# Down-projection phases of a fused attention and GLU kernel: halves with six weight buffers, or thirds with seven, and where the weight loads are placed

## The chip, the core and the metric

The kernel runs on one core of one Trainium2 chip. The metric is the device time of one execution in microseconds (us); lower is better.

## The reference

Four blocks follow each other on 2048 tokens of width 576, each with a layer norm ahead of it and a residual sum behind it. Blocks one and three are attention, blocks two and four a gated linear unit; both attention blocks share their weights, and so do both GLU blocks.

```python
def _A_ref(x, wqkv, wo):            # H = 32 heads of 18, window W = 8, dilation 2
    q, k, v = split(x @ wqkv)
    idx = pos[:, None] - arange(W) * 2
    logits = einsum("bhsd,bhswd->bhsw", q, k[idx]) * 18 ** -0.5     # masked where idx < 0
    o = einsum("bhsw,bhswd->bhsd", softmax(logits), v[idx])
    return merge_heads(o) @ wo

def _B_ref(x, w_gate, w_up, w_down):  # 576 -> 4608 -> 576
    return ((x @ w_gate) * (x @ w_up)) @ w_down

x = x + _A_ref(_layernorm(x), A_wqkv, A_wo)
x = x + _B_ref(_layernorm(x), B_w_gate, B_w_up, B_w_down)
x = x + _A_ref(_layernorm(x), A_wqkv, A_wo)
x = x + _B_ref(_layernorm(x), B_w_gate, B_w_up, B_w_down)
```

## The kernel before

**Steps.** The 16 token tiles of 128 go in two groups of eight, layer after layer. A step `j` is one attention and one GLU for one or two tiles (`nst`); the first four steps have one tile, the other 14 have two, 18 in all. Gate and up weights (`wg`, `wu`, `wgu_t`) stay in SBUF; the down weights (`wd`) are read again from HBM in every step, 18 loads of 288 KB a step.

**Order.** Nothing is issued where the source stands. Every piece of work is recorded by `op` with its engine, an assumed cost, and the keys that it reads and writes; `Plan.run` then issues all of them greedily by assumed start time, and that order is each engine's instruction stream. An engine works through its stream in order. A dependency exists where a key was written or read by an operation recorded *earlier*. The planner assumes a cost for DMAs too (`nbytes`, `late`), one queue at a time. The GLU matmuls of all steps form one chain (`bb`), so the attention's operations are fitted in between.

**The GLU.** A unit is 512 columns of gate and up: for two tiles, two of the 36 feature tiles, so 18 units a step. Three units form a group: `full` (L709) does the 128-row parts, `tails` (L720) the last 64 rows, into PSUM banks `pg` and `pu`, three of each. `evac` copies the gate to SBUF on ScalarE (L731) and multiplies on VectorE (L732); the result `h` goes into one of `NH` = 9 buffers. A bank is free again when that product is done. After nine units, a half (`nph` = 2 for two tiles), a down phase multiplies them by `wd` (L756, L757) into one bank of each kind and `acct`, and `settle` (L766, L771) adds the sums to the residual `xf`. One-tile steps have nine units and three phases of three.

**The loads.** There are `NWD` = 6 buffers `wd`. The first six loads are issued by SP, all others by GpSimd. In `glu`, the loads of three units are recorded ahead of their gate/up matmuls:

```python
for m in us:
    wsl[m] = [load_wd(m * fpu // 2 + g) for g in range(fpu // 2)]
...
for m in mine:
    down(m, hsl[m], wsl[m], ph, use)
```

All nine loads of a half are so recorded ahead of its down matmuls. Loads seven to nine take the buffers of the first three, and their only recorded dependency is on those loads and on the half before. They are issued as soon as that half's matmuls have freed the buffers.

**The attention.** `esel` (L568) sums the products of queries and keys per head, the softmax follows on VectorE and ScalarE (L590 to L601). Its weights must be spread over the partitions: from step 5 on L621 writes them to `a_dram`, and four reads at L624 bring them back as `ab`, all by SP's queue, which also has the transposing DMAs at L387. VectorE then multiplies values by `ab` (L641) and adds (L655), and TensorE projects with `wo` (L668).

Of the kernel before, what the change touches and what calls it, by code (L numbers as in the profile page):

```python
# [9 lines left out]
ACT = mybir.ActivationFunctionType  # L10
# [7 lines left out]
                 "lat", "margin", "ready", "end", "nbytes", "use", "pair", "need", "due", "late")  # L18


SLACK = {"DVE": 500, "ACT": 300}


class Plan:
# [11 lines left out]
    def op(self, eng, cost, fn, r=(), w=(), prio=1, after=None, hold=None, free=None, margin=0, nbytes=0, use=None,  # L36
           pair=None, need=None, due=False, late=0):
        o = Op()
        o.due, o.late = due, late
        o.eng, o.cost, o.fn, o.prio, o.hold, o.free = eng, cost, fn, prio, hold, free  # L40
        o.margin, o.idx, o.succ, o.order, o.nbytes = margin, len(self.ops), [], set(), nbytes
        o.lat, o.use, o.pair, o.need = self.LAT[eng], use, pair, need
        d = set()
        for k in r:
            d.update(self.wr.get(k, ()))
        for k in w:
            d.update(self.wr.get(k, ()))
            d.update(self.rd.get(k, ()))
        for k in r:
            self.rd.setdefault(k, []).append(o)  # L50
        for k in w:
            self.wr[k] = [o]
            self.rd[k] = []
        d.discard(o)
        o.deps = d
        if after is not None and after not in d:
            o.order.add(after)
        for p in d | o.order:
            p.succ.append(o)
        o.n = len(d | o.order)  # L60
        self.ops.append(o)
        return o
# [80 lines left out]
def kernel(  # L143
# [12 lines left out]
    nc = tc.nc  # L156
    _, S, D = A_x.shape
    F = B_w_gate.shape[1]
    P = 128
# [10 lines left out]
    NFT = F // P  # L170
# [3 lines left out]
    qscale = float(Dh) ** -0.5  # L174
    assert D == 576 and TL == 64 and NTT % (2 * GT) == 0 and NFT % 4 == 0 and nlayers % 2 == 0

    NXS, NWD, NH, NXB, NB = 4, 6, 9, 3, 3

    consts = ctx.enter_context(tc.tile_pool(name="consts", bufs=1))
    psum = ctx.enter_context(tc.tile_pool(name="psum", bufs=1, space=PSUM))  # L180
# [3 lines left out]
    wd_v = B_w_down.rearrange("(g t p) d -> g p t d", p=P, t=2)  # L184
# [36 lines left out]
    wd = [sb(f"wd{i}", [P, 2, D]) for i in range(NWD)]  # L221
# [3 lines left out]
    acct = psum.tile([P, 512], FP32, name="acct")  # L225
# [5 lines left out]
    late = {}  # L231

    pl = Plan()
    op = pl.op
# [120 lines left out]
    def head(src, keys, nst, dst, key, prio, ab, on_pe, mg, c0=0):  # L355

        mv, st, rstd, nmr, xn = mv_[ab], st_[ab], rstd_[ab], nmr_[ab], xn_[ab]
        ia = c0 // P
        for i in range(nst):
            def stats(i=i):  # L360
                xr = src(i).rearrange("p (a b) -> p a b", a=2)
                for a in range(2):
                    nc.vector.bn_stats(out=st[:, ia + i, a, :], in_=xr[:, a, :])
                nc.vector.bn_aggr(out=mv[:, ia + i, :], in_=st[:, ia + i])
            op("DVE", 970, stats, r=[keys[i]], w=[f"mv{ab}{ia + i}"], prio=prio)
        mk = [f"mv{ab}{ia + i}" for i in range(nst)]
        nk = [f"nmr{ab}{ia + i}" for i in range(nst)]
        sl = slice(ia, ia + nst)

        def rs():  # L370
            nc.scalar.activation(rstd[:, sl], mv[:, sl, 1], ACT.Ln, bias=eps_t[:])
            nc.scalar.activation(rstd[:, sl], rstd[:, sl], ACT.Exp, scale=-0.5)
        rk = [f"rstd{ab}{ia + i}" for i in range(nst)]
        op("ACT", 440, rs, r=mk + ["eps"], w=rk, prio=prio)
        op("DVE", 75, lambda: nc.vector.scalar_tensor_tensor(nmr[:, sl], mv[:, sl, 0], -1.0, rstd[:, sl], op0=ALU.mult, op1=ALU.mult),
           r=mk + rk, w=nk, prio=prio)
        for i in range(nst):
            def apply(i=i):
                x, y = src(i), xn[ia + i]
                sc = dict(bias=nmr[:, ia + i:ia + i + 1], scale=rstd[:, ia + i:ia + i + 1])  # L380
                nc.scalar.activation(y[:, 0:D], x, ACT.Identity, **sc)
                if not on_pe:
                    nc.scalar.activation(y[:, D:D + TL], x[:, KF * P:D], ACT.Identity, **sc)
            op("ACT", 770 if on_pe else 1100, apply, r=[keys[i], nk[i]], w=[f"xn{ab}{ia + i}"], prio=prio)
            cs = slice(c0 + i * P, c0 + (i + 1) * P)
            if not on_pe:
                op("SP", 1250, lambda i=i, cs=cs: nc.sync.dma_start_transpose(out=dst[:, :, cs], in_=xn[ia + i][:]),  # L387
                   r=[f"xn{ab}{ia + i}"], w=[key + str(ia + i)], prio=0, nbytes=P * KT * P * 2, late=3000)
                continue
            b = Bank()  # L390

            def tr(i=i, b=b):
                for k in range(KF):
                    nc.tensor.transpose(bf(b())[:, k, :], xn[ia + i][:, k * P:(k + 1) * P], ident[:])
                for r_ in (0, TL):
                    nc.tensor.transpose(bf(b())[r_:r_ + TL, KF, :], xn[ia + i][:, KF * P:D], ident[:])
            o = op("PE", 290, tr, r=[f"xn{ab}{ia + i}", "ident"], prio=0, margin=mg, **b.take())
            pl.also(o, [key + str(ia + i)])
            op("ACT", 590, lambda i=i, b=b, cs=cs: nc.scalar.copy(dst[:, :, cs], bf(b())), r=[b.key], w=[key + str(ia + i)],  # L399
               prio=prio, **b.drop())  # L400
# [277 lines left out]

    chain = {"pe": None}
    unit_no = {"n": 0}  # L680
    wd_no = {"n": 0}

    def fkeys(nm, fts):
        return sorted({f"{nm}{ft * FS // NFT}" for ft in fts})
# [1 line left out]
    def glu(j, t0, nst, last):  # L686
        n = nst * P
# [11 lines left out]
        def bb(eng, cost, fn, **kw):  # L699
            o = op(eng, cost, fn, prio=1, after=chain["pe"], **kw)  # L700
            chain["pe"] = o
            return o
# [30 lines left out]
               r=[f"wu_{j}_{u}", f"g{gs}"], w=[f"h{hs}"], prio=0, due=True, free="unit", use=use)  # L733
            return hs

        def load_wd(g):
            b = wd_no["n"] % NWD
            wd_no["n"] += 1
            first = wd_no["n"] <= NWD
            eng, q = ("SP", nc.sync) if first else ("POOL", nc.gpsimd)  # L740
            op(eng, 550 if first else 1100, lambda: q.dma_start(wd[b][:], wd_v[g]), w=[f"wd{b}"], nbytes=P * 2 * D * 2, late=0 if first else 1000,  # L741
               prio=5.5 + (g // 3 if j == 0 else 0))
            return b

        nph = 2 if nst == 2 else 3
        upp = nu // nph

        def down(u, hs, bl, ph, use):
            for e, ft in enumerate(fts(u)):
                first, fin = ft == ph * upp * fpu, ft == (ph + 1) * upp * fpu - 1  # L750

                def fn(e=e, ft=ft, first=first, fin=fin):
                    wt = wd[bl[e // 2]]
                    for i in range(nst):
                        lhs = hb[hs][:, e * n + i * P:e * n + (i + 1) * P]
                        nc.tensor.matmul((pg, pu)[i][use["slot"]][:], lhsT=lhs, rhs=wt[:, e % 2, 0:512], start=first, stop=fin)  # L756
                        nc.tensor.matmul(acct[:, i * TL:(i + 1) * TL], lhsT=lhs, rhs=wt[:, e % 2, 512:D],  # L757
                                         start=(first and i == 0), stop=fin, skip_group_check=True)
                kw = dict(hold="unit", use=use) if first else {}
                bb("PE", 245 * nst, fn, r=[f"h{hs}", f"wd{bl[e // 2]}"], w=["acc", "acct"], **kw)  # L760

        def settle(ph, use):
            fin = last and ph == nph - 1
# [12 lines left out]

        units = {}
        for ph in range(nph):
            hsl, wsl = {}, {}
            mine = range(ph * upp, (ph + 1) * upp)  # L780
            for u in range(ph * upp, (ph + 1) * upp, NB):
                us = (u, u + 1, u + 2)
                for m in us:
                    wsl[m] = [load_wd(m * fpu // 2 + g) for g in range(fpu // 2)]
                    units[m] = {}
                full(u, wg, "wg", pg, True, False, pair=tuple(units[m] for m in us))
                full(u, wu, "wu", pu, True, False)
                full(u + 1, wg, "wg", pg, True, False, need=units[u + 1])
                tails(us)
                hsl[u] = evac(u)  # L790
                full(u + 1, wu, "wu", pu, False, True)
                hsl[u + 1] = evac(u + 1)
                full(u + 2, wg, "wg", pg, False, True)
                full(u + 2, wu, "wu", pu, False, True)
                hsl[u + 2] = evac(u + 2)
            use = {"left": nst}
            for m in mine:
                down(m, hsl[m], wsl[m], ph, use)
            settle(ph, use)

    seq = []
# [13 lines left out]
    setup_b()  # L815
    setup_wo()
    setup_glu()
    for j, (l, t0, nst) in enumerate(seq):
        if l == 0 and j >= 4:
            load_x(t0, nst)  # L820
        pool["k"] = "pa" if j else "boot"
        attention(j, l, t0, nst)
        if j == 0:
            op("PE", 0, lambda: None, w=list(boot_keys), free="unit", use={"slot": NB - 1})
        glu(j, t0, nst, l == n_al - 1)
# [30 lines left out]
```

## Time and profile before

| | |
|---|---|
| median of 3 runs | 1116.48 us |
| lowest, highest | 1112.98, 1119.39 us |
| the profiled execution | 1110.56 us |
| its span | 1108.7 us |
| TensorE (PE) busy | 1058.9 us |
| VectorE (DVE) busy | 760.4 us |
| ScalarE (ACT), GpSimd (POOL) busy | 352.9, 242.7 us |
| read from HBM | 118.51 MB |
| mean granted TensorE clock | 0.99 |

Every duration below comes from the profiled execution, and its times are in us from the span's start unless marked ns. In the lists of waits a row names the engine and tile that waited, after the arrow the engine and tile that ended the wait, and then the total in us, the count and the longest. In timelines the brackets give the engine's idle time before the instruction and what ended it.

### The profile page before, as it was taken

The page shows a single profiled execution, that of the slowest core. Times are in us where ns is not written, and L with a number is a line of the kernel's source. Part 1 is how long each engine was busy: PE and PEld are TensorE (multiplying, and loading weights), DVE is VectorE, ACT ScalarE, POOL GpSimd, SP SyncE. Part 2 cuts the span into 40 slices and gives each one's busy share as a digit, 9 for nine tenths or more (in the row PEclk, how much of TensorE's full clock was granted, in tenths as well). Part 3 has the DMA queues.
Part 4 walks back from the last instruction along what each step waited for, and adds up shares of the span by engine and source line. Part 5 has one row for each costly group of instructions (what it writes and reads, how often), then busy time and mean ns, then how long its engine had stood idle before and what let it go on. Part 6 is the DMA issues. An engine that isn't in the chain of part 4 may idle for free.

```text
span 1108.7 us, 25201 instructions
## 1 busy us (share of the span) xinstructions
PE 1058.9 (96%) x10752; PEld 793.9 (72%) x10824; DVE 760.4 (69%) x1346; ACT 352.9 (32%) x704; POOL 242.7 (22%) x348
## 2 busy tenths in 40 slices
PE   6999999897989999999998999999999999999998
PEld 5777777775766677776776677777777777777775
DVE  7688989778787979888796533585877867322222
ACT  6633254331333353132332122225233232211211
POOL 4043433022202202222102222220222222222220
PEclk8999999998999999999999999999999999999999
DMA  9945654363336324463434334232343433333330
GB/s 302 284 162 172 196 155 129 87 125 115 90 56 144 88 69 120 121 135 108 97 90 121 119 97 120 68 122 54 121 121 109 118 87 121 99 102 114 98 119 31
DMA packets 84848, 132.74 MB, mean 120 GB/s; under 512 B 42048, under 2 KB 63744, under 8 KB 84736
## 3 DMA queue, kind: packets, MB, share of 16 engines
q0 software_dynamic: 25440, 93.80, 28.4%
q1 hardware_dynamic: 59296, 37.33, 13.6%
q8 instruction: 84, 1.38, 0.5%
q14 instruction: 28, 0.23, 0.1%
HBM read 118.51 MB, written 4.06 MB: 111 GB/s over the span
## 4 chain that ended last, share of the span: by engine, by line
PE 72%; DVE 16%; DMA 7%; issue 2%; ACT 1%; SPq 1%; POOL 0%; DVEq 0%; POOLq 0%; ACTq 0%
PE pu L709 18%; PE pg L709 18%; PE pg L756 9%; PE pu L756 7%; PE pg L720 5%; PE pg L455 5%; PE pu L455 3%; DVE prod L641 3%; PE pa L668 3%; PE acct L757 3%; DVE oT L655 3%; DMA ab<-a_dram 3%; DMA a_dram<-s 2%; DVE h L732 2%; DVE prod L553 2%
## 5 line engine op out<-in xcount | busy, mean ns | idle before, releaser
L741 POOL DMA_DIRECT2D wd<-in_B_w_down_dram x318 | 229.4, 723 | 836.2 <-PE acct L757 800.2
L731 ACT CAST g_sb<-pg 128x512 bf16<-128x512 f32 x288 | 158.9, 585 | 523.9 <-PE pu L720 361.9
L709 PE MATMUL pu<-xnT_B,wu 128*128 128x256 bf16 (+1 forms) x2592 | 301.6, 262 | 6.2 <-DVE h L732 6.2
L709 PE MATMUL pg<-xnT_B,wg 128*128 128x256 bf16 (+1 forms) x2592 | 300.5, 261 | 1.6 <-ACT xnT_B L399 1.6
L732 DVE TENSOR_TENSOR h<-pu,g_sb 128x512 bf16<-128x512 f32 x288 | 193.3, 685 | 139.2 <-ACT g_sb L731 87.1
L709 PEld LDWEIGHTS <-wu 128*128 128x128 bf16 x2592 | 224.3, 98 | 47.0 <-issue 23.6
L709 PEld LDWEIGHTS <-wg 128*128 128x128 bf16 x2592 | 229.1, 98 | 29.9 <-issue 1.5
L757 PE MATMUL acct<-wd,h 128*128 128x64 bf16 x1152 | 222.7, 193 | 4.0 <-issue 0.4
L756 PE MATMUL pg<-wd,h 128*128 128x512 bf16 x605 | 218.0, 382 | 0.1
L756 PEld LDWEIGHTS <-h 128*128 128x128 bf16 x1152 | 113.3, 98 | 132.7 <-issue 3.2
L756 PE MATMUL pu<-wd,h 128*128 128x512 bf16 x475 | 181.9, 383 | 6.7 <-DVE h L732 6.7
L757 PEld LDWEIGHTS <-h 128*128 128x128 bf16 x1152 | 113.3, 98 | 7.8 <-issue 6.9
L455 PEld LDWEIGHTS <-wqkv 128*128 128x128 bf16 (+1 forms) x1260 | 100.1, 101 | 26.0 <-issue 15.5
L553 DVE TENSOR_TENSOR prod<-qT,kv 128x2560 bf16<-128x2560 bf16 (+1 forms) x68 | 90.0, 1326 | 24.3 <-ACT kv L497 23.3
L655 DVE TENSOR_TENSOR oT<-oT,prod 128x1280 bf16<-128x1280 bf16 (+1 forms) x119 | 91.1, 765 | 3.6
L641 DVE TENSOR_TENSOR prod<-kv,ab 128x1280 bf16<-128x1280 bf16 (+1 forms) x120 | 88.3, 738 | 2.1 <-PE pg L646 1.9
L720 PE MATMUL pu<-xnT_B,wgu_t 64*128 64x256 bf16 (+1 forms) x648 | 80.5, 260 | 4.1 <-DVE h L732 3.8
L455 PE MATMUL pg<-xnT_A,wqkv 128*128 128x256 bf16 (+3 forms) x650 | 80.8, 267 | 2.5 <-DMA xnT_A<-xn 1.7
L720 PE MATMUL pg<-xnT_B,wgu_t 64*128 64x256 bf16 (+1 forms) x648 | 80.5, 260 | 0.0
L455 PE MATMUL pu<-xnT_A,wqkv 128*128 128x256 bf16 (+3 forms) x610 | 78.0, 268 | 0.1
L766 DVE TENSOR_TENSOR xf<-pg,xf 128x512 f32<-128x512 f32 (+1 forms) x40 | 27.3, 683 | 72.0 <-PE pg L756 70.8
L720 PEld LDWEIGHTS <-wgu_t 64*128 64x128 bf16 x1296 | 50.7, 94 | 28.4 <-issue 23.2
(99 smaller groups left out, 665.0 us busy)
## 6 DMA issues: line engine op xcount, KB each, us to landing
wd<-in_B_w_down_dram POOLq DMA_DIRECT2D x318, 288.0 KB, 4.5
ab<-a_dram SPq DMA_DIRECT2D x52, 128.0 KB, 2.8
wg<-in_B_w_gate_dram SPq DMA_DIRECT2D x6, 768.0 KB, 9.3
wu<-in_B_w_up_dram SPq DMA_DIRECT2D x6, 768.0 KB, 10.4
out_dram<-xf SPq DMA_DIRECT2D x8, 288.0 KB, 5.4
wraw<-in_A_wqkv_dram SPq DMA_DIRECT2D x4, 432.0 KB, 4.7
wd<-in_B_w_down_dram SPq DMA_DIRECT2D x6, 288.0 KB, 8.3
xb<-in_A_x_dram SPq DMA_DIRECT2D x6, 288.0 KB, 3.3
```

Of the source, the lines that this page charges most:

```text
L455: nc.tensor.matmul(bank(p_, u)[0:m, e * n:(e + 1) * n], lhsT=wqkv[r_, k, w0:w0 + m], rhs=xnT_A[r_, k, c0:c0 + n], start=start, stop=stop, ...
L553: nc.vector.tensor_tensor(late["prod"][p_ % 2][:, :, :, 0:n], q2, k2, op=ALU.mult)
L641: nc.vector.tensor_tensor(js(dst), js(vT[:, :, o0:o0 + n]), abw, op=ALU.mult)
L655: op("DVE", 70 + 2.63 * n, lambda i_=i_: nc.vector.tensor_tensor(oT[:, :, 0:n], oT[:, :, 0:n], late["prod"][i_ % 2][:, 0, :, 0:n], op=ALU. ...
L668: nc.tensor.matmul(b()[:, 0:HD], lhsT=oT[:, t, i * P:(i + 1) * P], rhs=wo_p[:, t, hh * HD:(hh + 1) * HD], start=(t == 0), stop=(t == KT - 1))
L709: nc.tensor.matmul(pt[:, e * n:(e + 1) * n], lhsT=w_[:, k, ft * P:(ft + 1) * P], rhs=xT[:, k, 0:n], start=(first and k == 0 and e == 0), s ...
L720: nc.tensor.matmul(ps[:, e * n:(e + 1) * n], lhsT=wgu_t[r_, ft * P:(ft + 1) * P], rhs=xT[r_, KF, 0:n], start=(first and e == 0), stop=not ...
L731: op("ACT", 490, lambda: nc.scalar.copy(g_sb[gs][:, 0:ul], pg[use["slot"]][:, 0:ul]), r=[f"wg_{j}_{u}"], w=[f"g{gs}"], prio=0, due=True)
L732: op("DVE", 605, lambda: nc.vector.tensor_tensor(hb[hs][:, 0:ul], pu[use["slot"]][:, 0:ul], g_sb[gs][:, 0:ul], op=ALU.mult), r=[f"wu_{j}_{ ...
L741: op(eng, 550 if first else 1100, lambda: q.dma_start(wd[b][:], wd_v[g]), w=[f"wd{b}"], nbytes=P * 2 * D * 2, late=0 if first else 1000, p ...
L756: nc.tensor.matmul((pg, pu)[i][use["slot"]][:], lhsT=lhs, rhs=wt[:, e % 2, 0:512], start=first, stop=fin)
L757: nc.tensor.matmul(acct[:, i * TL:(i + 1) * TL], lhsT=lhs, rhs=wt[:, e % 2, 512:D], start=(first and i == 0), stop=fin, skip_group_check=True)
```

## The change

Two-tile steps get three down phases of six units instead of two of nine (`nph = 3` for all steps), so `NH` = 6 buffers for `h` suffice. There are `NWD` = 7 buffers for down weights. A counter `used` walks through the buffers in the order of the down matmuls; when the two feature tiles of a load have been recorded, the next load into that buffer is recorded right behind them, so it depends on exactly these matmuls. Seven loads are recorded ahead of everything and go by SP, the other 317 by GpSimd. The operation that applies the layer norm (L381) is now also a reader of `rstd`.

```diff
+POOLQ = True
-    NXS, NWD, NH, NXB, NB = 4, 6, 9, 3, 3
+    NXS, NWD, NH, NXB, NB = 4, 7, 6, 3, 3
...
-            op("ACT", 770 if on_pe else 1100, apply, r=[keys[i], nk[i]], w=[f"xn{ab}{ia + i}"], prio=prio)
+            op("ACT", 770 if on_pe else 1100, apply, r=[keys[i], nk[i], rk[i]], w=[f"xn{ab}{ia + i}"], prio=prio)
...
-    wd_no = {"n": 0}
+    wd_no = {"n": 0, "used": 0}
+
+    def load_wd():
+        i = wd_no["n"]
+        wd_no["n"] += 1
+        if i >= len(seq) * NFT // 2:
+            return
+        b, first = i % NWD, i < NWD
+        eng, q = ("SP", nc.sync) if first or not POOLQ else ("POOL", nc.gpsimd)
+        op(eng, 550 if first else 1100, lambda: q.dma_start(wd[b][:], wd_v[i % (NFT // 2)]), w=[f"wd{b}"], nbytes=P * 2 * D * 2,
+           late=0 if first else 1000, prio=5.5 + (i // 3 if first else 0))
...
-        def load_wd(g):
-            b = wd_no["n"] % NWD
-            wd_no["n"] += 1
-            first = wd_no["n"] <= NWD
-            eng, q = ("SP", nc.sync) if first else ("POOL", nc.gpsimd)
-            op(eng, 550 if first else 1100, lambda: q.dma_start(wd[b][:], wd_v[g]), w=[f"wd{b}"], nbytes=P * 2 * D * 2, late=0 if first else 1000,
-               prio=5.5 + (g // 3 if j == 0 else 0))
-            return b
-
-        nph = 2 if nst == 2 else 3
+        nph = 3
...
-        def down(u, hs, bl, ph, use):
+        def down(u, hs, ph, use):
...
+                wb = wd_no["used"] % NWD
...
-                bb("PE", 245 * nst, fn, r=[f"h{hs}", f"wd{bl[e // 2]}"], w=["acc", "acct"], **kw)
+                bb("PE", 245 * nst, fn, r=[f"h{hs}", f"wd{wb}"], w=["acc", "acct"], **kw)
+                if e % 2:
+                    wd_no["used"] += 1
+                    load_wd()
...
-                    wsl[m] = [load_wd(m * fpu // 2 + g) for g in range(fpu // 2)]
...
+    for _ in range(NWD):
+        load_wd()
     for j, (l, t0, nst) in enumerate(seq):
```

More of the change, by code (lines that the diff above doesn't have):

```diff
@@ L734, in evac, with fn @@
             return hs
-        def load_wd(g):
-            b = wd_no["n"] % NWD
-            wd_no["n"] += 1
-            first = wd_no["n"] <= NWD
-            eng, q = ("SP", nc.sync) if first else ("POOL", nc.gpsimd)
-            op(eng, 550 if first else 1100, lambda: q.dma_start(wd[b][:], wd_v[g]), w=[f"wd{b}"], nbytes=P * 2 * D * 2, late=0 if first else 1000,
-               prio=5.5 + (g // 3 if j == 0 else 0))
-            return b
-        nph = 2 if nst == 2 else 3
+        nph = 3
         upp = nu // nph
-        def down(u, hs, bl, ph, use):
+        def down(u, hs, ph, use):
             for e, ft in enumerate(fts(u)):
                 first, fin = ft == ph * upp * fpu, ft == (ph + 1) * upp * fpu - 1
-                def fn(e=e, ft=ft, first=first, fin=fin):
-                    wt = wd[bl[e // 2]]
+                wb = wd_no["used"] % NWD
+                def fn(e=e, ft=ft, first=first, fin=fin, wb=wb):
+                    wt = wd[wb]
                     for i in range(nst):
@@ L778, in glu @@
         for ph in range(nph):
-            hsl, wsl = {}, {}
+            hsl = {}
             mine = range(ph * upp, (ph + 1) * upp)
@@ L797, in glu @@
             for m in mine:
-                down(m, hsl[m], wsl[m], ph, use)
+                down(m, hsl[m], ph, use)
             settle(ph, use)
```

## The prediction

> **What bounds the kernel now.** I read the page first, then the waits, then the timelines of DVE, SP and POOL around the longest TensorE waits, and at last the windows behind them. `h` is the product that DVE writes at L732; the bounce is the DMA round trip by which the attention weights are spread over partitions (L621 writes `a_dram`, four reads at L624 bring it back as `ab`).
>
> ```profile
> span 1108.7 us, 25201 instructions
> PE 1058.9 (96%) x10752; PEld 793.9 (72%) x10824; DVE 760.4 (69%) x1346; ACT 352.9 (32%) x704; POOL 242.7 (22%) x348
> ```
>
> TensorE is busy for 96%. Its work is the same before and after, so only the 50 us in which it stands still, and what follows from them, are to be had. The waits name their causes:
>
> ```profile
> PE pu L756 <- DVE h L732: 6.7, 2, 5.6
> PE pu L709 <- DVE h L732: 6.2, 2, 3.5
> PE pu L720 <- DVE h L732: 3.8, 2, 2.0
> PE pa L668 <- DVE xf L674: 3.4, 4, 1.5
> PE pa L668 <- DVE oT L655: 3.2, 4, 1.2
> DVE oT L641 <- DMA ab<-a_dram: 50.1, 12, 7.8
> ```
>
> Six waits for `h` make 16.7 us. Why is `h` late? Around the longest:
>
> ```profile
> 246.17 0.69 DVE L732 TENSOR_TENSOR h<-pu,g_sb 128x512 bf16<-128x512 f32 x1 [1.05 <-PE pu L709]
> 254.17 0.83 DVE L641 TENSOR_TENSOR oT<-kv,ab 128x1280 bf16<-128x1280 bf16 x1 [7.32 <-DMA ab<-a_dram]
> 257.25 1.28 DVE L732 TENSOR_TENSOR h<-pu,g_sb 128x512 bf16<-128x512 f32 x2
> ```
> ```profile
> 241.20 0.36 SPq L621 DMA_DIRECT2D a_dram<-s  x1
> 249.90 1.75 SPq L624 DMA_DIRECT2D ab<-a_dram  x4
> ```
> ```profile
> 228.72 0.72 POOL L741 DMA_DIRECT2D wd<-in_B_w_down_dram  x1 [33.49 <-PE acct L757]
> 233.62 2.16 POOL L741 DMA_DIRECT2D wd<-in_B_w_down_dram  x3 [0.26 <-PE acct L757]
> 236.96 0.72 POOL L741 DMA_DIRECT2D wd<-in_B_w_down_dram  x1 [1.18 <-DMA wd<-in_B_w_down_dram]
> ```
>
> DVE executes in order. The first multiplication by `ab` sits in its queue and waits 7.3 us for the bounce; the next `h`, whose PSUM bank has long been filled, stands behind it, and TensorE runs out of free banks. The bounce is late because nine down-weight loads went out in the 9 us from 228.7, ahead of it: the `a_dram` write alone took until 249.9. Without loads beside it the bounce takes 6.0 us (L601 ends at 403.97, `ab` is used at 410.01):
>
> ```profile
> 403.29 0.68 DVE L601 TENSOR_TENSOR s<-Lt,zs 128x512 bf16<-128x512 f32 x1
> 410.01 0.81 DVE L641 TENSOR_TENSOR oT<-kv,ab 128x1280 bf16<-128x1280 bf16 x1
> ```
>
> A long wait costs more than itself, since the granted clock falls to half behind it (the row after each wait; PE, PEld, DVE, ACT and POOL busy, then PEclk, DMA share, GB/s):
>
> ```profile
> 252.40:258.00 5.60, 0.03 (x2) 0.01 (x1) 3.79 (x6) 0.00 (x0) 0.00 (x0) 0.88 0.11 25
> 258.00:263.50 5.50, 5.28 (x22) 2.35 (x23) 5.43 (x8) 0.59 (x1) 0.00 (x0) 0.50 0.00 0
> 309.90:314.70 4.80, 4.76 (x34) 3.12 (x34) 4.73 (x7) 1.66 (x3) 0.00 (x0) 0.64 0.83 59
> 606.00:608.70 2.70, 0.04 (x1) 0.03 (x1) 2.67 (x5) 0.00 (x0) 0.00 (x0) 0.91 0.00 2
> 608.70:611.60 2.90, 2.90 (x14) 1.98 (x14) 2.90 (x5) 0.59 (x1) 0.00 (x0) 0.50 0.00 0
> ```
>
> Lost to the clock: 5.5 x 0.50 + 4.8 x 0.36 + 2.9 x 0.50 = 2.8 + 1.7 + 1.5 = 5.9 us. With the waits, **22.6 us** hang on late bounces, at five places: 4.5 us a place.
>
> The Trainium skill (TensorE: Matmul & The Clock Gate, Part 1: The HAM clock gate) has the clock fall after at least one idle window of about 3.4 us. The trace is stricter: 2.70 us were enough before 608.7. By the page's rule alone that place would have kept its clock, and the 22.6 us would be 21.1.
>
> **The change, part by part.** *Thirds instead of halves.* Each of the 14 two-tile steps gets one more down phase and one more settle. TensorE's matmuls stay; the question is the seam.
>
> ```profile
> 959.00:967.82 8.82, 8.71 (x72) 4.54 (x72) 0.76 (x2) 0.00 (x0) 3.40 (x5) 1.00 0.31 88
> 977.40:982.75 5.35, 5.35 (x50) 4.62 (x50) 2.08 (x3) 1.33 (x3) 0.00 (x0) 1.00 0.01 3
> ```
>
> A down of nine units takes 8.82 us, 0.98 a unit, and runs between two gate/up blocks with TensorE busy throughout; the 48 gate/up matmuls that follow each other across two groups of three units take 5.35. A third is thus two such groups and a down of 5.9 us, and the extra seam costs 0. What hides it: the last `h` of a third has 5 x 0.98 = 4.9 us of down matmuls ahead of it, against the 0.69 us of the `h` rows above and an ACT copy of a like size. If an `h` is late by more, it is the case counted below.
>
> ```profile
> L766 DVE TENSOR_TENSOR xf<-pg,xf 128x512 f32<-128x512 f32 (+1 forms) x40 | 27.3, 683 | 72.0 <-PE pg L756 70.8 <-PE acct L757 1.0
> L766 DVE TENSOR_TENSOR xf<-pu,xf 128x512 f32<-128x512 f32 (+1 forms) x28 | 19.1, 681 | 0.0
> L771 DVE TENSOR_TENSOR xf<-acct,xf 128x128 f32<-128x128 f32 (+2 forms) x40 | 10.6, 264 | 0.8
> ```
> ```profile
> 330.00:440.00 110.00, 105.02 (x984) 77.58 (x990) 92.91 (x163) 44.84 (x94) 19.47 (x27) 1.00 0.42 106
> ```
>
> The 14 settles add 14 x (0.68 + 0.68 + 0.26) = 23 us to DVE, which has 348 us idle. They stand in its queue where TensorE is in a down and no `h` is due (that row shows DVE waiting 70.8 us for down ends already). I take 0; at most the 1.6 us of a settle delay attention work in the stretch where DVE is busiest (92.9 us of the 110 above); five of the 14 steps run there, at some 65 us a step from 220 to 550: 8 us. Less than 0 is excluded, since they are added work.
>
> *The loads.* Their number stays 324, seven instead of six by SP at the start. Each is now placed behind the matmuls that free its buffer, so nothing is queued behind it on GpSimd but the next load.
>
> ```profile
> L741 POOL DMA_DIRECT2D wd<-in_B_w_down_dram x318 | 229.4, 723 | 836.2 <-PE acct L757 800.2 <-DMA wd<-in_B_w_down_dram 24.0 <-PE pa L668 7.1
> DMA to landing us min/median/max: 3.2/4.6/12.3
> ```
>
> A buffer freed in one third is read seven units on, behind at least the two gate/up groups of a third, 10.7 us; landing takes 4.6 us, at worst 12.3, and that in a burst of nine. So TensorE waits for no weight: 0, as before, where no wait for `wd` is listed. The seventh load by SP delays the last two of six gate/up slices by 1.4 us (0.29 MB at the 211 GB/s shown below); the first tile reads them in its last third: 0. `NH` 9 to 6 costs 0, since a third has six `h` and the next third's first comes behind all its downs. The added `rk` only lengthens a chain that `nmr` had already: 0.
>
> *The bursts.* This is the term that counts. A down now releases six loads in 5.9 us, not nine in 9. I read in the built program where each of the 13 bounces stands. Five begin inside a down, as at 296 before; three begin just behind one; five stand clear of any. In one of the first five the `ab` multiplication precedes the next `h` directly; in four, two `h` stand ahead of it.
>
> ```profile
> 295.25 0.69 DVE L601 TENSOR_TENSOR s<-Lt,zs 128x512 bf16<-128x512 f32 x1
> 307.73 0.82 DVE L641 TENSOR_TENSOR oT<-kv,ab 128x1280 bf16<-128x1280 bf16 x1 [7.04 <-DMA ab<-a_dram]
> 190.60 0.69 DVE L601 TENSOR_TENSOR s<-Lt,zs 128x512 bf16<-128x512 f32 x1
> 202.32 0.82 DVE L641 TENSOR_TENSOR oT<-kv,ab 128x1280 bf16<-128x1280 bf16 x1 [4.45 <-DMA ab<-a_dram]
> 588.41 0.69 DVE L590 TENSOR_REDUCE mx<-pa 128x64 f32<-128x512 f32 x1 [0.96 <-PE pa L568]
> 592.18 0.69 DVE L601 TENSOR_TENSOR s<-Lt,zs 128x512 bf16<-128x512 f32 x1
> ```
> ```profile
> DMA packets 1591, 3.17 MB, mean 211 GB/s; under 512 B 418, under 2 KB 1058, under 8 KB 1591
> ab<-a_dram SPq DMA_DIRECT2D x4, 128.0 KB, 7.0
> ```
>
> The second fence is the DMA of 294 to 309 us. The bounce there took 307.73 - 295.94 = 11.8 us with nine loads. Three loads fewer are 0.88 MB, 4.2 us at the 211 GB/s shown; they were issued together with the `ab` reads, so about half of that stood before these: 2.0 us less, **9.8 us**, between the quiet 6.0 and the 11.8. The direct case: 11.8 us gave a wait of 3.5, so it waits from 8.3 on: 1.5 us now, too short for the clock (bounds 0 and 5.2). The case with two `h` ahead: 202.32 - 191.29 = 11.0 gave 2.0, so it waits from 9.0 on where the bounce began 1 us before the next gate/up block. In three of the four, the `esel` matmuls stand 16 gate/up matmuls (1.8 us) and a down (5.9) ahead of that block; from `esel`'s end to L601's end is 4.5 us (588.4 to 592.9), so the bounce begins 3.2 us before it, and the fourth no later. That moves the point to about 11. I take 0.5 each, nearer to 0 than to 2.0: 2.0 us. The three behind a down meet only the end of a burst and have three or five `h` ahead: 0.
>
> Sum: -22.6 + 1.5 + 2.0 = **-19.1 us**. The waits at L668 (6.6 us) I leave as they are. The profiled execution took 1110.6 us, 5.9 below the median of 1116.5 and below the lowest of the three; its own time becomes 1091.5, the median **1097**.
>
> **The rivals.**
> *The crossings cost what they did.* Five places remain inside a down. If `ab` suffers from any load beside it and not from their number, five times 4.5 us return: 0 gained, 1116. For it: at 296 only two or three loads were out when `a_dram` was written, and `ab` still took 7.0, more than the whole quiet bounce. Against: two `h` stand ahead in four of the five. The Trainium skill (DMA: Bandwidth & Descriptors, Queues, rings and completion order) lets each DMA engine take turns between queue rows packet by packet, so that a transfer would share with whatever the other row holds, however long that is; the 8.7 us of the `a_dram` write at 241, behind bursts that had been issued, speak against that alone.
>
> *Slower: bursts come oftener.* There are 42 downs instead of 28 in these steps, and eight bounces begin in one or just behind one. If the three behind a down are caught as the one at 241 was (it began after the down's last matmul), eight places cost 4.5 us: 36 against 22.6, +13.6, 1130. It decides when bounces of more than five places pass 11 us.
>
> *DVE's settles reach the path.* With the 8 us above: -11, 1105.
>
> **How the numbers follow.** Forecast 0.62, with its own range 1089 to 1107 (left-over waits of 0 to 13 us at the five places, and 3 us for a median); settles 0.08; crossings as dear as before 0.14, at 1113 to 1119; slower 0.16. The range 1089 to 1119 leaves out the last and a little below. A measurement of this kernel can tell about 0.5%, 5.6 us, from no change: faster is forecast and settles, 0.70; same 0.14; slower 0.16.
>
> **What would show it.** Right: the waits of TensorE for `h` sum below 6 us; the granted clock stays at 1.00 between 60 and 1100 us; bounces in a down take near 10 us; no wait for `wd`; L766 has 68 + 28 instructions; GpSimd issues at most six loads in a row. Wrong: waits for `h` of 17 us or more, bounces over 11 us, or new waits at L756 where a third's last `h` is late.

## The result and the profile after

The changed kernel took 1104.92 us (median of 4 runs, 1102.47 to 1107.09) against 1116.61 for the kernel before: a ratio of 0.9897, 95% interval 0.9861 to 0.9933. It is faster by 11.7 us; 19 were forecast. The two profiled executions lie only 4.8 us apart (1110.56 and 1105.75): the one before took less than any of the four runs behind its median (1112.98 to 1119.39), and an experiment below profiles that kernel again.

The page of the changed kernel, first lines:

```profile
span 1104.0 us, 25345 instructions
PE 1056.1 (96%) x10757; PEld 792.2 (72%) x10824; DVE 778.4 (71%) x1388; ACT 352.3 (32%) x704; POOL 242.3 (22%) x347
```

Its waits follow. Most lines stand 1 to 11 lower in the source than before (the loads moved from L741 up to L691), so L720 and L731 are the gate/up matmuls and their tails, L759 the down matmuls, L669 the projection with `wo`, L743 `h`, L772 the settle, L642 and L656 the multiplication by `ab` and its sum, L456 the projection of queries, keys and values:

```profile
DVE oT L642 <- DMA ab<-a_dram: 38.4, 13, 7.1
PE pa L669 <- DVE oT L656: 8.4, 9, 2.2
PE pg L456 <- DMA xnT_A<-xn: 5.1, 3, 2.3
PE pu L720 <- DVE h L743: 2.9, 1, 2.9
PE pg L731 <- DVE xf L772: 2.1, 2, 1.2
PE pa L669 <- DVE xf L675: 1.8, 3, 0.9
PE pu L759 <- DVE h L743: 0.8, 1, 0.8
PE pu L731 <- DVE xf L772: 0.7, 2, 0.3
PE pu L456 <- DVE h L743: 0.5, 1, 0.5
```

TensorE's waits for `h` fell from 16.7 us to 4.2. But it waits longer for `oT` (3.2 to 8.4), for the transposed activations (1.7 to 5.1) and for the settle (0.3 to 2.8). Its span less its busy time, which is all its idle time, shrank from 49.8 to 47.9 us only; most of the rest of the 4.8 us came from the clock.

A bounce inside a down, with the loads that it meets (VectorE's timeline, then GpSimd's; the first columns are start and duration):

```profile
296.38 0.69 DVE L602 TENSOR_TENSOR s<-Lt,zs 128x512 bf16<-128x512 f32 x1
307.99 0.82 DVE L642 TENSOR_TENSOR oT<-kv,ab 128x1280 bf16<-128x1280 bf16 x1 [7.12 <-DMA ab<-a_dram]
```
```profile
295.02 0.72 POOL L691 DMA_DIRECT2D wd<-in_B_w_down_dram  x1 [12.80 <-PE acct L760]
...
299.93 0.72 POOL L691 DMA_DIRECT2D wd<-in_B_w_down_dram  x1 [0.26 <-PE acct L760]
```

Six loads go out 1 us apart, and nothing follows them. From the end of L602 (297.07) to L642 the bounce takes 10.9 us. By the same reading the five bounces that begin inside a down (at 297, 349, 494, 546 and 593 us) take 10.9, 9.1, 11.0, 8.5 and 10.1 us, a mean of 9.9.

Where the time reappears is seen behind the longest of them (VectorE, then TensorE):

```profile
493.15 0.69 DVE L602 TENSOR_TENSOR s<-Lt,zs 128x512 bf16<-128x512 f32 x1
504.88 0.82 DVE L642 TENSOR_TENSOR oT<-kv,ab 128x1280 bf16<-128x1280 bf16 x1 [3.06 <-DMA ab<-a_dram]
...
516.64 0.82 DVE L656 TENSOR_TENSOR oT<-oT,prod 128x1280 bf16<-128x1280 bf16 x1
```
```profile
517.52 0.79 PE L669 MATMUL pa<-wo_p,oT 128*128 128x288 bf16 x5 [2.22 <-DVE oT L656]
```

No `h` was late here. The chain of multiplications and sums that starts with `ab` started late, ended late at 517.46, and the `wo` matmul, which stands in TensorE's order where the planner expected `oT`, waited 2.2 us. And the granted clock (the third number from the right) fell behind that wait as it did behind the 2.9 us for `h`:

```profile
309.50:313.60 4.10, 4.10 (x28) 2.59 (x27) 4.07 (x7) 1.25 (x3) 0.00 (x0) 0.59 0.00 0
517.50:521.80 4.30, 4.06 (x21) 2.53 (x23) 4.25 (x6) 1.06 (x2) 0.00 (x0) 0.61 0.00 0
```

It was 0.50 for 3.4 us in each of the two rows and 1.00 in the rest of them. The loss is 4.1 x 0.41 + 4.3 x 0.39 = 3.4 us, against 5.9 before.

### The profile page after: what moved, and what is told of

It is laid out like the page before. It is cut to its first block, busy times and chain, and to the rows that moved or that the text cites. A ratio compares the mean times of both kernels' runs of the same rounds, so it can differ in the third digit from the quotient of the medians.

```text
span 1104.0 us, 25345 instructions
## 1 busy us (share of the span) xinstructions
PE 1056.1 (96%) x10757; PEld 792.2 (72%) x10824; DVE 778.4 (71%) x1388; ACT 352.3 (32%) x704; POOL 242.3 (22%) x347
## 4 chain that ended last, share of the span: by engine, by line
PE 64%; DVE 20%; DMA 9%; issue 3%; ACT 2%; SPq 1%; DVEq 0%
PE pu L720 17%; PE pg L720 16%; PE pg L759 8%; PE pu L759 6%; PE pg L731 5%; DVE oT L656 4%; DVE prod L642 4%; PE pg L456 4%; DVE h L743 3%; DMA a_dram<-s 3%; DMA ab<-a_dram 3%; PE pu L456 3%; PE acct L760 3%; PE pa L669 2%; DMA xnT_A<-xn 2%
## 5 line engine op out<-in xcount | busy, mean ns | idle before, releaser
L691 POOL DMA_DIRECT2D wd<-in_B_w_down_dram x317 | 228.9, 723 | 837.8 <-PE acct L760 834.0
L720 PE MATMUL pu<-xnT_B,wu 128*128 128x256 bf16 (+1 forms) x2592 | 301.0, 261 | 2.9 <-DVE h L743 2.9
L720 PE MATMUL pg<-xnT_B,wg 128*128 128x256 bf16 (+1 forms) x2592 | 300.3, 261 | 1.6 <-ACT xnT_B L400 1.6
L743 DVE TENSOR_TENSOR h<-pu,g_sb 128x512 bf16<-128x512 f32 x288 | 193.0, 685 | 126.7 <-ACT g_sb L742 76.0
L720 PEld LDWEIGHTS <-wu 128*128 128x128 bf16 x2592 | 224.3, 98 | 42.7 <-issue 20.1
L720 PEld LDWEIGHTS <-wg 128*128 128x128 bf16 x2592 | 228.2, 98 | 31.3 <-issue 1.8
L759 PE MATMUL pg<-wd,h 128*128 128x512 bf16 x590 | 210.1, 381 | 0.0
L759 PEld LDWEIGHTS <-h 128*128 128x128 bf16 x1152 | 113.0, 98 | 129.1 <-issue 1.3
L759 PE MATMUL pu<-wd,h 128*128 128x512 bf16 x495 | 188.6, 381 | 1.0 <-DVE h L743 0.8
L456 PEld LDWEIGHTS <-wqkv 128*128 128x128 bf16 (+1 forms) x1260 | 99.0, 100 | 30.1 <-issue 17.5
L656 DVE TENSOR_TENSOR oT<-oT,prod 128x1280 bf16<-128x1280 bf16 (+1 forms) x119 | 90.9, 764 | 3.2
L642 DVE TENSOR_TENSOR prod<-kv,ab 128x1280 bf16<-128x1280 bf16 (+1 forms) x120 | 88.0, 736 | 2.1 <-PE pg L647 1.9
L456 PE MATMUL pg<-xnT_A,wqkv 128*128 128x256 bf16 (+3 forms) x650 | 80.4, 266 | 5.9 <-DMA xnT_A<-xn 5.1
L772 DVE TENSOR_TENSOR xf<-pg,xf 128x512 f32<-128x512 f32 (+1 forms) x54 | 36.7, 679 | 65.6 <-PE pg L759 63.6
L731 PE MATMUL pg<-xnT_B,wgu_t 64*128 64x256 bf16 (+1 forms) x648 | 80.7, 260 | 2.1 <-DVE xf L772 2.1
L731 PE MATMUL pu<-xnT_B,wgu_t 64*128 64x256 bf16 (+1 forms) x648 | 80.4, 260 | 0.7 <-DVE xf L772 0.7
L456 PE MATMUL pu<-xnT_A,wqkv 128*128 128x256 bf16 (+3 forms) x610 | 77.0, 266 | 0.6 <-DVE h L743 0.5
L731 PEld LDWEIGHTS <-wgu_t 64*128 64x128 bf16 x1296 | 50.7, 94 | 27.0 <-issue 21.7
```

Source lines behind the costliest of these rows:

```text
L456: nc.tensor.matmul(bank(p_, u)[0:m, e * n:(e + 1) * n], lhsT=wqkv[r_, k, w0:w0 + m], rhs=xnT_A[r_, k, c0:c0 + n], start=start, stop=stop, ...
L642: nc.vector.tensor_tensor(js(dst), js(vT[:, :, o0:o0 + n]), abw, op=ALU.mult)
L656: op("DVE", 70 + 2.63 * n, lambda i_=i_: nc.vector.tensor_tensor(oT[:, :, 0:n], oT[:, :, 0:n], late["prod"][i_ % 2][:, 0, :, 0:n], op=ALU. ...
L720: nc.tensor.matmul(pt[:, e * n:(e + 1) * n], lhsT=w_[:, k, ft * P:(ft + 1) * P], rhs=xT[:, k, 0:n], start=(first and k == 0 and e == 0), s ...
L731: nc.tensor.matmul(ps[:, e * n:(e + 1) * n], lhsT=wgu_t[r_, ft * P:(ft + 1) * P], rhs=xT[r_, KF, 0:n], start=(first and e == 0), stop=not ...
L743: op("DVE", 605, lambda: nc.vector.tensor_tensor(hb[hs][:, 0:ul], pu[use["slot"]][:, 0:ul], g_sb[gs][:, 0:ul], op=ALU.mult), r=[f"wu_{j}_{ ...
```

## The experiments

Two theories of the gain stood at first: the shorter burst of loads lets the bounce come back sooner; or the new order and placement did it, whatever the loads do.

**Thirds alone**, on the kernel before:

```diff
-        nph = 2 if nst == 2 else 3
+        nph = 3
```

> The kernel before with thirds alone (nph = 3; six weight buffers, nine h buffers and the recording of the loads stay, six loads fill a third's six buffers). Burst theory (a shorter burst of loads lets the bounce come back sooner, so h is late less often): the bursts have six loads as in the changed kernel, so the time falls as there, 1105 +- 5 us, TensorE's waits for h sum to 3 to 8 us, bounces inside a down take 8.5 to 11 us. Placement theory (the gain is from loads behind their matmuls and the seventh buffer): 1112 to 1120 us, waits for h of 15 us or more.

L381 is not recorded as a reader of `rstd` here, as in the kernel before; in the order that results one step's layer norm takes another step's scale. The amount of work is the same.

1104.88 us (1102.02 to 1105.83), ratio 0.9889, interval 0.9865 to 0.9914. TensorE's waits:

```profile
PE pa L668 <- DVE oT L655: 9.3, 8, 2.2
PE pg L709 <- DVE xf L766: 3.1, 1, 3.1
PE pu L756 <- DVE h L732: 2.4, 2, 1.2
PE pu L455 <- DVE h L732: 1.9, 2, 1.3
PE pu L720 <- DVE h L732: 0.5, 2, 0.3
```

The waits for `h` are 4.8 us and the time is that of the changed kernel: the thirds make the whole gain. As in the changed kernel, TensorE waits longer for `oT` and for a settle (3.1 us). The placement, the seventh buffer and the three buffers fewer for `h` add nothing to it.

**The placement alone**, the changed kernel with halves:

```diff
-    NXS, NWD, NH, NXB, NB = 4, 7, 6, 3, 3
+    NXS, NWD, NH, NXB, NB = 4, 6, 9, 3, 3
-        nph = 3
+        nph = 2 if nst == 2 else 3
```

> The changed kernel with halves (nph = 2 for two tiles, nine h buffers, six weight buffers since seven don't fit beside nine h): the placement alone. Loads of units 7 to 9 can go out only when the downs of units 1 to 3 are done, 5.9 us before they are read, against 4.6 us of median landing and up to 12.3 in a burst. Burst theory: nothing is gained, waits for h as before (10 us or more), and the 28 halves add waits for wd at the down matmuls of 0.5 to 3 us each: 1125 to 1190 us. Placement theory: at or below 1110 us.

1127.18 us, ratio 1.0103 (1.0076 to 1.0131): slower, in the range of the burst theory, but its waits are others than expected:

```profile
PE pa L569 <- DVE s L563: 10.5, 7, 2.2
PE pa L669 <- DVE oT L656: 8.9, 9, 1.4
PE pg L759 <- DMA wd<-in_B_w_down_dram: 6.2, 6, 3.0
```

The down weights cost 6.2 us in six places, not 14 and more in 28. The largest new wait is that of `esel` for VectorE. The planner ordered the attention differently, probably because it now counts on weights that come later; neither that nor why it costs 10 us was followed further. So with halves the placement costs 10 us, and with thirds it neither costs nor gains.

**No loads**, in the changed kernel and in the kernel before:

```diff
-lambda: q.dma_start(wd[b][:], wd_v[i % (NFT // 2)])
+lambda: first and q.dma_start(wd[b][:], wd_v[i % (NFT // 2)])
```

> The changed kernel with the 317 loads by GpSimd left out (the down matmuls read the seven first tiles over and over, so the output is not the reference's); the order on TensorE, VectorE, ScalarE and SyncE is the same. Burst theory: all 13 bounces near 6 us, waits for h below 1 us, no clock loss after 60 us, and the waits for oT at L669 and for xnT_A at L456 shrink too, since both follow from the same DMAs: 1088 to 1096 us. Order theory (the planner's order of VectorE's work against the gate/up units costs the time, whatever the loads do): 1101 to 1108 us with the waits where they were.

> The kernel before with the 318 loads by GpSimd left out (output not the reference's); the order on the other engines is the same. Burst theory: the 22.6 us that hang on late bounces go, bounces near 6 us: 1088 to 1096 us, within 4 us of the changed kernel without loads, so the order itself is worth nothing. Order theory: 1110 us or more, and some 10 us above the changed kernel without loads.

1083.75 us (1082.65 to 1084.78) and 1082.88 us (1082.32 to 1084.04), both below the expected 1088 to 1096. Without loads the two orders take the same time within 1 us. What the loads cost, in waits and in the clock behind them, is 1104.92 - 1083.75 = 21.2 us in the changed kernel and 1116.68 - 1082.88 = 33.8 us in the kernel before, the median of the same session. The difference, 12.6 us, less the 0.9 us between the two orders, is the whole gain: the change loses less to the loads. Of the changed kernel's waits at L669 these are left without loads:

```profile
PE pa L669 <- DVE xf L675: 2.4, 4, 0.9
PE pa L669 <- DVE oT L656: 1.2, 4, 0.5
```

There is no wait for `h`, none for the DMA that transposes into `xnT_A`, and 1.2 us for `oT` instead of 8.4. So in the changed kernel those waits, too, come from DMAs that are late beside loads.

**The kernel before, profiled again.**

> The kernel before, unchanged, profiled once more: does the profile that the prediction was made from show a usual execution? Its own time was 5.9 us below the median. If the late bounces vary from execution to execution, this one shows 1112 to 1119 us, the same order, and more than the 22.6 us of h waits and clock loss that were read there; if not, the waits are the same within 3 us and the difference to the median lies elsewhere.

1122.73 us, in one execution; this is above the expected 1112 to 1119 us and above seven unprofiled runs taken with it (1114.36 to 1121.99):

```profile
PE pu L709 <- DVE h L732: 10.5, 2, 6.5
PE pu L756 <- DVE h L732: 6.4, 1, 6.4
PE pu L720 <- DVE h L732: 4.9, 2, 2.8
```
```profile
297.14 0.69 DVE L601 TENSOR_TENSOR s<-Lt,zs 128x512 bf16<-128x512 f32 x1
312.37 0.82 DVE L641 TENSOR_TENSOR oT<-kv,ab 128x1280 bf16<-128x1280 bf16 x1 [10.03 <-DMA ab<-a_dram]
```

The order is the same and the places are the same, but the bounce that took 11.8 us takes 14.5 here, and the waits for `h` are 21.8 us instead of 16.7. TensorE stands idle for 56.3 us instead of 49.8, and the same matmuls keep it busy for 1064.6 us instead of 1058.9, at a mean granted clock of 0.982 instead of 0.990. So the bounces change in length from execution to execution of one order, and in these two the time goes with them. Two profiles do not show that this makes the whole spread of the kernel before.

**The loads spaced out**, in the changed kernel. GpSimd clears a buffer `pace` of 128x384 four times behind each load from the 81st on, so in nearly all of the two-tile steps:

```diff
+        def fn():
+            q.dma_start(wd[b][:], wd_v[i % (NFT // 2)])
+            for _ in range(4 if i >= 80 else 0):
+                nc.gpsimd.memset(pace[:], 0.0)
```

> The changed kernel with GpSimd clearing a small buffer four times behind each load of the two-tile steps, so loads go out some 2.3 us apart instead of 1 us; bytes and the order on the other engines are the same. Burst theory: a load or two beside a bounce instead of six, bounces 6.5 to 8.5 us, half or more of the 21 us that the loads still cost goes: 1089 to 1097 us. Presence theory (any load beside the bounce costs the same, whatever their number): bounces stay at 8.5 to 11 us, and more of them are met: 1103 to 1112 us.

1106.73 us (1103.99 to 1112.47), ratio 0.9895: no gain, in the range of the presence theory. The loads do go out 2.7 us apart, and the five bounces in a down get shorter (a mean of 8.6 us, not 9.9). But those that begin some 10 us behind the end of a down, where the changed kernel's burst has long gone out, get longer, as this one:

```profile
295.43 0.72 POOL L694 DMA_DIRECT2D wd<-in_B_w_down_dram  x1 [3.98 <-PE acct L766]
...
298.10 0.72 POOL L694 DMA_DIRECT2D wd<-in_B_w_down_dram  x1
```
```profile
783.40 0.69 DVE L603 TENSOR_TENSOR s<-Lt,zs 128x512 bf16<-128x512 f32 x1
795.12 0.83 DVE L643 TENSOR_TENSOR oT<-kv,ab 128x1280 bf16<-128x1280 bf16 x1 [7.18 <-DMA ab<-a_dram]
```

11.0 us, where the changed kernel's bounce at that place took 9.2. From the end of the attention weights' product to the landing of the last `ab` read, the 13 bounces add up to 108 us in the changed kernel and to 106 us with spaced loads; without loads they add up to 82. In these profiles, one execution of each, spacing moved the delay and did not remove it.

**The planner told of the delay**, in the changed kernel and in the kernel before:

```diff
-nbytes=P * W * sq * 2, late=1200)
+nbytes=P * W * sq * 2, late=4200)
```

> The changed kernel with the planner told that the ab reads land 3 us later (late=4200 instead of 1200 at L625), so the multiplication by ab is planned later and more h products and gate/up units stand ahead of it, and the wo matmuls are planned later too. If the 21 us left are waits behind a bounce that the planner thinks is faster than it is, the waits for oT at L669 and for h fall below 5 us together: 1092 to 1099 us. If the DMA contention slows TensorE's chain whatever the order, 1102 to 1108 us.

> The kernel before (halves, six buffers, nine-load bursts) with the planner told that the ab reads land 3 us later (late=4200). Planner theory (what the bursts cost is the difference between the bounce that happens and the bounce that the planner counts on): h waits below 5 us and 1086 to 1096 us, so the shorter bursts of the change are one of two ways to the same end. Burst theory in its first form (nine loads in a row are themselves the cost): the bounces of 11 to 14 us still overrun the 12.4 us or so now planned, 1098 to 1110 us.

1085.55 us (1084.49 to 1086.29) for the changed kernel, ratio 0.9698 (0.9661 to 0.9736): 19 us below the changed kernel as it stood, and below both expected ranges. Its waits for the bounce and for what follows it:

```profile
DVE oT L642 <- DMA ab<-a_dram: 4.6, 4, 3.1
PE pa L669 <- DVE xf L675: 1.4, 3, 0.8
PE pa L669 <- DVE oT L656: 1.3, 3, 0.6
```
```profile
401.10 0.69 DVE L602 TENSOR_TENSOR s<-Lt,zs 128x512 bf16<-128x512 f32 x1
...
405.40 0.69 DVE L743 TENSOR_TENSOR h<-pu,g_sb 128x512 bf16<-128x512 f32 x1 [2.01 <-ACT g_sb L742]
406.27 0.69 DVE L743 TENSOR_TENSOR h<-pu,g_sb 128x512 bf16<-128x512 f32 x1 [0.18 <-PE pu L720]
408.02 0.69 DVE L743 TENSOR_TENSOR h<-pu,g_sb 128x512 bf16<-128x512 f32 x1 [1.05 <-PE pu L720]
411.78 0.82 DVE L642 TENSOR_TENSOR oT<-kv,ab 128x1280 bf16<-128x1280 bf16 x1 [3.07 <-DMA ab<-a_dram]
```

Bounces of 10 us still occur, as the one from 401.79 to 411.78, but three `h` are done ahead of it, and TensorE waits for none. So 19 of the 21 us were not bandwidth that TensorE lacks but the difference between the bounce that comes and the bounce that the planner counts on.

The kernel before with the same number took 1098.49 us (1091.60 to 1101.76), ratio 0.9823 (0.9774 to 0.9872): better by 19, and still 13 us behind. That is the edge of the second range, though the waits for `h` are only 1.0 us, as the planner theory had it. In its profile, which is of the slowest of the four runs, a bounce overruns the later time as well (VectorE's timeline, then SyncE's queue, then TensorE's waits):

```profile
293.92 0.68 DVE L601 TENSOR_TENSOR s<-Lt,zs 128x512 bf16<-128x512 f32 x1
311.71 0.83 DVE L641 TENSOR_TENSOR oT<-kv,ab 128x1280 bf16<-128x1280 bf16 x1 [6.96 <-DMA ab<-a_dram]
```
```profile
292.12 2.56 SPq L387 DMA_TRANSPOSE xnT_A<-xn  x2
294.77 0.56 SPq L621 DMA_DIRECT2D a_dram<-s  x1
307.39 1.73 SPq L624 DMA_DIRECT2D ab<-a_dram  x4
```
```profile
PE pg L455 <- DMA xnT_A<-xn: 8.3, 4, 4.4
PE pa L668 <- DVE oT L655: 7.5, 5, 5.8
```

That bounce took 17.1 us, 12.6 of them in the `a_dram` write. Six loads had gone out just ahead of it, from 291.0 us on, but two transposes too, in the write's own queue; they landed at 301.2 and 304.3 us, so the delay is not shown to be the loads' alone. What sets the two kernels apart, the burst of nine loads among it, thus counts with the later time as well: the change brings 12 us with the short time in the planner and 13 with the long one.

**Spacing and the later time together.**

> Both of the above together. If pacing and the planner's later time take the same waits, no better than the better of the two (within 3 us); if they are separate, near the 1084 us of the kernel without loads, 1086 to 1092 us.

1084.09 us (1083.32 to 1086.59) against 1085.55: the ranges overlap, so beside the planner's time the spacing shows no gain of its own.

**The transposes' time raised as well.**

```diff
-nbytes=P * KT * P * 2, late=3000)
+nbytes=P * KT * P * 2, late=6000)
```

> The changed kernel with the planner told that the ab reads land 3 us later and the transposes at L388 3 us later too (6000 instead of 3000). The kernel with the first alone has one wait of 3.2 us for xnT_A left, and the kernel without loads took 1083.8: if the transposes' waits are late DMAs of the same kind, 1080 to 1085 us; if moving them costs as much elsewhere, 1085 to 1090 us.

1088.25 us (1086.93 to 1089.74), ratio 0.9736 (0.9696 to 0.9776), in the second range. The interval overlaps that of the later bounce time alone (0.9661 to 0.9736), so no gain is shown, and no loss either. The wait for `xnT_A` is gone, and 1.8 us for down weights and more for other transposed tiles came in its place:

```profile
PE pg L720 <- ACT xnT_B L400: 2.9, 2, 2.1
PE pa L395 <- ACT xnT_B L400: 2.7, 1, 2.7
PE pg L759 <- DMA wd<-in_B_w_down_dram: 1.8, 1, 1.8
```

## Why the prediction was right, and where it was off

- **The mechanism** (loads delay the bounce, the bounce holds `h` back, TensorE waits) is shown by the kernels without loads, in which no wait for `h` is left. That thirds help by shorter bursts is less sure. Thirds also change the order, and with it how many `h` stand ahead of a late bounce. Spacing the loads with the order kept gained nothing; another order with the same loads gained 19 us in either kernel. How much of the 12 us is the burst's and how much the order's was not separated.
- **What held the bounce.** The prediction laid the 8.7 us of the `a_dram` write at 241.2 to the nine loads alone. Two transposes had gone out ahead of it by the same queue, SyncE's, and the second landed at 246.0 (the row below). In all traces here seven `a_dram` writes took more than 6 us, and each had a transpose of its own queue in flight when it went out; without one the longest took 5.6. Without loads a write behind a transpose took at most 1.9 us. So the loads are needed for the delay, but part of it may come through the transposes that they make late.

```profile
231.66 3.67 SPq L387 DMA_TRANSPOSE xnT_B<-xn  x2
```

- **The seam and the settles at 0**: shown within 1 us. Without loads, thirds take 1083.75 us and halves 1082.88. VectorE's 18 us more (760.4 to 778.4, where 23 were forecast) cost nothing by themselves.
- **No wait for down weights**: right; no such wait stands in the list.
- **Bounces of 9.8 us in a down**: measured 9.9 on the mean, 8.5 to 11.0. **Waits of 3.5 us left for `h`**: measured 4.2. The direct case was forecast at 1.5 us and took 2.9, long enough for the clock.
- **"The waits at L668 I leave as they are"** is the step that failed. They went from 6.6 to 10.2 us; with them the waits for `xnT_A` rose by 3.4, those for the settle by 2.5. The clock lost 3.4 us where 0 was forecast, and the start was 0.8 us slower (45.5 us busy in the first 60, not 46.3). Together with the 0.7 on `h` that is 3.6 + 3.4 + 2.5 + 3.4 + 0.8 + 0.7 = 14.4, which within 0.1 us is the difference between the 19.1 forecast and the 4.8 between the two profiled executions. I had counted a late bounce only where `h` stands behind it. VectorE's chain behind a late `ab` is late whether or not an `h` stands in it, and what TensorE needs next from VectorE, `oT` or a settled bank, is late with it. Of the signs named in advance, the clock of 1.00 throughout is the one that failed; one bounce of 11.0 us and a wait of 0.8 us for `h` at the down matmuls touched the signs of being wrong.
- **From profile to median.** -22.6 us were read from an execution that lost less than usual. In the medians the loads cost the kernel before 33.8 us, and the change took 12.6 of them. The two errors partly cancelled: the term was too small, and the share that goes was too large. That the median still came out within the range is in part luck.
- **The rivals.** "Bursts come oftener" was half right: in the profile seven bounces meet a load before and 11 after, and three of the 11 (at 790, 858 and 925 us) stand clear of the down before them but run into the loads of the next, which the prediction did not count. But the longest got shorter, from 13 to 11 us, and the 13 in sum (to the landing of `ab`) went from 114 to 108 us. "The crossings cost what they did" fell with the waits for `h`. The packet-by-packet sharing that the Trainium skill describes (DMA: Bandwidth & Descriptors, Queues, rings and completion order) would fit the spaced loads: 12 bounces are 1 us or more longer than at the same place without loads, against nine in the changed kernel, and the sum is hardly smaller. The 8.7 us write at 241 and the 17.1 us bounce speak for or against it only in so far as the transposes ahead of them are not the cause. Which of the shared parts sets this was not measured.

## What to carry to other kernels

When a wait shrinks, follow the late operation's engine past the first waiter: the lateness belongs to everything behind it in that queue, and TensorE meets it at the next place. In a kernel whose order comes from assumed costs, compare the assumed time of a DMA round trip with the traced one first; here one number was worth 19 us, more than the rebuilt phases. And take a second profile of a kernel whose runs spread by half a per cent before pricing its waits from the first.

## What the runs showed of the hardware that was not expected

TensorE's granted clock fell to 0.50 from 518.4 to 521.8 us behind a wait of 2.2 us in the changed kernel; another of 2.2, at 417, left it at 1.00. That is shorter than the 2.7 of the prediction and than the window of about 3.4 us that the Trainium skill gives (TensorE: Matmul & The Clock Gate, Part 1: The HAM clock gate). In the changed kernel without loads it was 0.50 from 191.4 to 194.9 us with no longer wait just before than two of 0.8 us, among transposes by TensorE. And 288 KB loads spaced 2.7 us apart delayed a 128 KB round trip as much in sum as loads 1 us apart: 106 against 108 us over 13 bounces, 82 without any, in one execution of each.
